# Turning q and k by the DMA crossbar in place of TensorE, in batches 2 to 7 of an attention and SwiGLU kernel

## The chip, the cores and the metric

The kernel runs on one core of one Trainium2 chip. The time is device microseconds (us) of that core, from the first to the last instruction, as the median of several runs. Runs of one kernel mostly agree within a few tenths of a per cent; a run over 1.5% above the fastest of the same kernel counts as slow and is left out of the ratios. A ratio is the mean time of one kernel's fast runs over the mean of the other's fast runs of the same rounds on the same chip, so it is not quite the ratio of the medians that are quoted beside it.

Names: PE is TensorE (PEld its weight loads), DVE is VectorE, ACT is ScalarE, POOL is GpSimd, SP is SyncE. ACTq, POOLq and SPq are the sequencers of those engines, which issue DMAs. "L123" is a line of the kernel; lines of the changed kernel stand about 17 higher than those of the kernel before.

## The reference, cut to what matters

```python
batch, n_heads, seq, head_dim = (8, 8, 576, 64)          # q, k: randn * 0.1
scores = scale * np.matmul(q, k.transpose(0, 1, 3, 2))   # scale = 1/8
scores = np.where(causal, -1e9, scores + decay)          # decay[i, j] = cum[i] - cum[j]
attn = softmax(scores)                                   # written out in the reference
x = np.matmul(attn, v)                                   # heads side by side: [4608, 512]
out = (silu(x @ w_gate) * (x @ w_val)) @ w_out           # d_ff = 1536
```

All inputs are float32. The score matmul contracts over head_dim, so q and k must lie with head_dim on the partitions, that is, turned.

Of the kernel before, what the change touches and what calls it, by code (L numbers as in the profile page):

```python
# [9 lines left out]
BF16 = mybir.dt.bfloat16  # L10
# [22 lines left out]
def kernel(ctx, tc, q, k, v, f, w_gate, w_val, w_out, out):  # L33
    nc = tc.nc
    B, H, S, D = q.shape
# [3 lines left out]
    P = 128  # L39
# [26 lines left out]
    ps_o = ctx.enter_context(tc.tile_pool(name="ps_o", bufs=1, space=PSUM))  # L66
    dec_dram = nc.dram_tensor("dec_d", (BH, 2, 4, S), BF16, kind="Internal").ap()
    rc_dram = nc.dram_tensor("rc_d", (BH // GH + AHEAD * H // GH, GH * S), F32, kind="Internal").ap()
    order = ctx.enter_context(tc.manual_schedule())

    NBUF = 4
    FB = H // 2

    QK = [consts.tile([KR, 4, NB * P], BF16, name=f"QK{i}") for i in range(NBUF)]

    BF = {(nm, i): consts.tile([P, QT, 2, D], BF16, name=f"b_{nm}{i}") for nm in "qk" for i in range(2)}
    VB = [consts.tile([P, NB, 2, P], BF16, name=f"VB{i}") for i in range(NBUF)]
# [7 lines left out]
    def load(p, nm, part=0):  # L85
        if nm != "v":

            t = natp.tile([QP, 2, QT * D], F32, name=f"nat_{nm}", tag=f"nat_{nm}")
            nc.sync.dma_start(
                out=t, in_=srcs[nm][2 * p : 2 * p + 2].rearrange("h (p t) d -> p h (t d)", t=QT)  # L90
            )
            nat[nm, p] = t
            return
        if part == 0:
            nat[nm, p] = natp.tile([P, NB, 2, D], F32, name="nat_v", tag="nat_v", bufs=3)
        t = nat[nm, p]
        if part < 2:
            nc.sync.dma_start(
                out=t[:, : NB - 1, part, :],
                in_=srcs[nm][2 * p + part, : (NB - 1) * P].rearrange("(n p) d -> p n d", p=P),  # L100
            )
        else:
            nc.sync.dma_start(
                out=t[:LAST, NB - 1],
                in_=srcs[nm][2 * p : 2 * p + 2, (NB - 1) * P :].rearrange("h p d -> p h d"),
            )

    def rows(p):
        nc.sync.dma_start(
# [44 lines left out]
    def qk(h, i):  # L154
        b, j = (h // 2) % NBUF, h % 2
        ahead = h < AHEAD * H and i == 0
        if ahead:
            PT[h, 0] = pt0p.tile([P, 2 * QSPLIT], BF16, name="pt0", tag="pt0")
        elif i == 0 or (h < AHEAD * H and i == 1):
            PT[h, 0] = PT[h, 1] = ptp.tile([P, PT_W], BF16, name="pt", tag="pt")  # L160
        pt = PT[h, min(i, 1)]
        pool, tag = (ps_ffn, "f") if h < H and ahead else (ps_s, "s")
        s = pool.tile([P, 512], F32, name="s", tag=tag)
        c = 0
        for kt, q0, w in BANKS[i]:
            nc.tensor.matmul(  # L166
                s[:, c : c + w], QK[b][:, 2 * j + 1, kt * P : (kt + 1) * P], QK[b][:, 2 * j, q0 : q0 + w],
                start=True, stop=True,
            )
            c += w  # L170
        off = OFFS[i]
        nc.scalar.activation(pt[:, off : off + c], s[:, :c], AF.Exp, scale=0.125)  # L172
        if i == 0:
            diag = pt[:, : 2 * QSPLIT].rearrange("p (n x) -> p n x", x=QSPLIT)[:, :, :P]
            pat = [[0, 2], [1, P]]
        else:
            kt, q0, w = [x for x in BANKS[i] if x[1] == x[0] * P][0]
            lo = off + sum(x[2] for x in BANKS[i][: [y[0] for y in BANKS[i]].index(kt)])
            m = min(P, w)
            diag, pat = pt[:, lo : lo + m], [[1, m]]  # L180
        nc.gpsimd.affine_select(  # L181
            out=diag, in_=diag, pattern=pat, compare_op=ALU.is_ge, fill=0.0, base=0, channel_multiplier=-1,
        )
# [140 lines left out]
    with tc.tile_pool(name="ini", bufs=1) as ini:  # L324
        lf = ini.tile([BH, S], F32, name="lf")
        nc.scalar.dma_start(out=lf, in_=f.rearrange("b h s -> (b h) s"))
        for p in range(2):
            load(p, "q")
            load(p, "k")
        for part in range(3):  # L330
            load(0, "v", part)
        for part in range(3):
            load(1, "v", part)
        load(2, "q")
        load(2, "k")
        ident = consts.tile([P, P], BF16, name="ident")
        make_identity(nc, ident[:, :])
        ident_f = consts.tile([P, P], F32, name="ident_f")
        zero = ini.tile([BH, S], F32, name="zero")
        dec = ini.tile([BH, 2, 4, S], BF16, name="dec")  # L340
        nc.gpsimd.memset(zero, 0.0)
        for n in range(2):
            nc.vector.memset(BF["q", n][QP:], 0.0)
            nc.vector.memset(BF["k", n][QP:], 0.0)
        nc.vector.memset(dec[:, 1, 0], 1.0)
        nc.gpsimd.memset(dec[:, 0, 1:], 1.0)
        blanks(0)
        cast(0, "q")
        cast(0, "k")
        nc.vector.tensor_scalar(out=lf, in0=lf, scalar1=1e-4, scalar2=1.0, op0=ALU.max, op1=ALU.min)  # L350
        nc.scalar.activation(lf, lf, AF.Ln)
        idle(7)
        transposes(0, "q")
        straighten(0, "q", 0, nc.scalar)
        straighten(0, "q", 1, nc.scalar)
        idle(2)
        cast(1, "q")
        cast(1, "k")
        cum = ini.tile([BH, S], F32, name="cum")

        def row(r):

            nc.sync.dma_start(out=QK[0][D + r : D + r + 1, :, :S], in_=dec[0:2, :, r])

        nc.vector.tensor_tensor_scan(out=cum, data0=lf, data1=zero, initial=0.0, op0=ALU.add, op1=ALU.add)
        nc.scalar.activation(dec[:, 0, 0], cum, AF.Copy, scale=8.0)
        row(0)
        nc.vector.tensor_scalar_mul(dec[:, 1, 1], cum, -8.0)
        row(1)
        transposes(0, "k")  # L370
        straighten(0, "k", 0, nc.scalar)
        straighten(0, "k", 1, nc.scalar)
        r1 = ini.tile([BH, S], F32, name="r1")
        nc.vector.scalar_tensor_tensor(out=r1, in0=cum, scalar=-8.0, in1=dec[:, 1, 1], op0=ALU.mult, op1=ALU.subtract)
        nc.vector.tensor_copy(dec[:, 1, 2], r1)
        row(2)
        nc.vector.tensor_sub(dec[:, 1, 3], r1, dec[:, 1, 2])
        row(3)
        nc.sync.dma_start(out=dec_dram[:H], in_=dec[:H])

        warm = ini.tile([1, 1], F32, name="warm")
        nc.scalar.activation(warm, cum[:1, :1], AF.Exp)
        idle(4)
        transposes(1, "q")
        straighten(1, "q", 0, nc.scalar)
        straighten(1, "q", 1, nc.scalar)
        idle(2)
        cast(0, "v")
        transposes(1, "k")
        straighten(1, "k", 0, nc.vector)  # L390
        straighten(1, "k", 1, nc.vector)
        idle(3)
        load(3, "q")
        load(3, "k")
        for part in range(3):
            load(2, "v", part)
        rows(1)
        rows(2)
        rows(3)
        cast(2, "q")  # L400
        cast(2, "k")
        blanks(1)
        nc.gpsimd.tensor_copy(ident_f, ident)
        blanks(2)
        nc.sync.dma_start(out=dec_dram[H:], in_=dec[H:])
    fp = ctx.enter_context(tc.tile_pool(name="fp", bufs=3))
# [52 lines left out]
    for p in range(NP):  # L459
        s0 = slot(2 * p, 0)  # L460
        if p >= AHEAD * FB:
            l, r = s0 - 20, s0 - 16
            cq, tq, ck, tk, cv = s0 - 12, s0 - 8, s0 - 8, s0 - 4, s0 - 4
        elif p >= FB:

            e = slot(2 * (p - NBUF) + 1, NSLOT - 1)
            l = (4, 7, 15, 19)[p - FB]
            r = e + 1
            tq = max(18 + 4 * (p - FB), e)
            tk = tq + 2  # L470
            cq, ck = tq - 4, tk - 4
            cv = e + LAG + 1
            lv = 8 + 5 * (p - FB)
        else:
            if p > 1:
                for nm, t in (("q", s0 - 3), ("k", s0 - 2)):
                    if p > 2:
                        at(s0 - 5, cast, p, nm)
                    at(t, transposes, p, nm)
                    for a in range(2):  # L480
                        at(t + a, straighten, p, nm, a, nc.scalar if nm == "q" else nc.vector)
            if p > 0:
                at(s0, cast, p, "v")
            continue
        for n, (nm, part) in enumerate((("q", 0), ("k", 0), ("v", 0), ("v", 1), ("v", 2))):
            at(l + n + n // 2 if p >= AHEAD * FB else l if n < 2 else lv, load, p, nm, part)
        at(r, rows, p)
        for nm, c, t in (("q", cq, tq), ("k", ck, tk)):
            at(c, cast, p, nm)
            at(t, transposes, p, nm)  # L490
            for a in range(2):
                at(t + a, straighten, p, nm, a, nc.scalar if nm == "q" else nc.vector)
        at(cv, cast, p, "v")
# [69 lines left out]
```

## The kernel before: what the change and the argument touch

Work goes by head pairs (32 of them, `p`), and by slots: each slot is one bank of scores of one head, and FFN matmuls of an earlier batch fill PE between slots. `at(slot, fn, ...)` puts a step into the program order of its engine at that slot. A pair has 8 slots, and `s0` is its first.

Before, q and k of a pair are loaded in float32 by SP, cast to bf16 by POOL, turned by PE into PSUM (six transposes for a pair's q, six for its k) and copied into the operand by ACT and DVE. Four extra rows of the operand (64 to 67) hold the decay, loaded by `rows`.

```python
QK = [consts.tile([KR, 4, NB * P], BF16, name=f"QK{i}") for i in range(NBUF)]   # KR = 68, NBUF = 4

def rows(p):
    nc.sync.dma_start(out=QK[p % NBUF][D:KR, :, :S], in_=dec_dram[...])

def transposes(p, nm):
    ...
    for n in range(QT):                                   # QT = 6
        nc.tensor.transpose(t[:, n * QP : n * QP + P], src[:, n], ident)

def straighten(p, nm, a, eng):                            # PSUM to operand, on ACT or DVE
    ...
```

The second part is the chain that divides by the softmax sums, once for every four heads. Its three DMAs are issued by ACT:

```python
def collect(x, g, lo, n):      # sums of four heads to 128 partitions
    nc.scalar.dma_start(out=SC[x][:, :c], in_=E[g][D : D + 1, ...])
def recip(x, n):
    nc.vector.reciprocal(RC[x][:, :c], SC.pop(x)[:, :c])
def back(x, n):                # reciprocals to DRAM
    nc.scalar.dma_start(out=rc_dram[x, : GH * n]..., in_=RC.pop(x)[:, :c])
def spread(x, n):              # broadcast of 576 KB to 64 partitions
    nc.scalar.dma_start(out=RB[x][:, : GH * n], in_=rc_dram[x, : GH * n]...to_broadcast(...))
def normalise(...):            # DVE: xT = ev * rb; the FFN of that batch waits for xT
    ...
```

One fact about the program that the source does not show, but its list of waits does: the framework gives the DMAs of the two hardware queues, SP's and ACT's together, eight completion semaphores in turn. Before a DMA is issued, its sequencer waits until the DMA that used the same semaphore last, eight DMAs back in program order, has landed. DMAs issued by POOL have eight others.

The softmax here doesn't subtract the row's maximum and nothing guards it: scores larger than these inputs give would overflow.

## Time and profile before

| | before |
|---|---|
| time, median | 451.91 us (451.03 to 453.86, 3 runs) |
| PE busy | 418.1 us, 93% of the span |
| DVE, ACT, POOL busy | 64%, 59%, 39% |
| granted PE clock, mean | 0.973 |

The page's second part cuts the span into 40 slices; a digit is the busy share in tenths. For the kernel before:

```profile
PE   8399587899899899999999999999999999999996
...
PEclk9758999999999999999999999999999999999999
DMA  9899960762818644942594359425912222200201
```

After the first fifth PE is full nearly everywhere. The table by stretches of time says it in numbers (columns: stretch, its length, busy us of PE, PEld, DVE, ACT and POOL with counts, granted clock, DMA share, GB/s; a DMA share adds up the times of all packets over 16 engines, so it can pass 1):

```profile
core 0: us, PE busy (x) PEld busy (x) DVE busy (x) ACT busy (x) POOL busy (x), PEclk, DMA share, GB/s
...
155.00:200.00 45.00, 43.40 (x312) 25.67 (x310) 32.57 (x56) 32.56 (x69) 23.36 (x54) 1.00 0.56 133
200.00:245.00 45.00, 45.00 (x306) 25.74 (x305) 31.41 (x51) 31.73 (x65) 20.29 (x48) 1.00 0.55 132
245.00:290.00 45.00, 45.00 (x308) 25.77 (x306) 31.32 (x51) 31.72 (x66) 20.27 (x48) 1.00 0.55 132
```

PE is busy 45.00 of 45 us, DVE and ACT about 31, the others less: PE is the limit here. What one group of six transposes costs PE is read from the timeline (start, length, engine, line):

```profile
202.98 0.50 PE L135 MATMUL tp<-ident,b_k 128*128 128x128 bf16 x6
203.32 0.81 PE L293 MATMUL gp<-xT,wg 128*128 128x512 bf16 x3
```

The group is listed as 0.50 us, but the next matmul starts 0.34 us after its first: the rest overlaps.

### The profile page before, as it was taken

To read this page: it belongs to the slowest core of one execution; us is meant where nothing else is said; L and a number is where in the kernel's file an instruction comes from. 1 tells how busy PE (TensorE), PEld (TensorE's weight loads), DVE (VectorE), ACT (ScalarE), POOL (GpSimd) and SP (SyncE) were. 2 spreads that over 40 slices of the span, in tenths; PEclk is the share of its full clock that TensorE was granted. 3 is DMA by queue.
4 is the path that set the end of the run, shared out by engine and by line. 5 is a ranking of instruction groups with operands and counts; after the bars stand their busy time and mean duration, and the time that the engine had idled before them with its cause. 6 is when DMAs were issued, how large, how long until landed. Compare 5 with 4: busy or idle time off the path is not lost.

```text
span 449.0 us, 8044 instructions
## 1 busy us (share of the span) xinstructions
PE 418.1 (93%) x2818; PEld 248.2 (55%) x2818; DVE 289.1 (64%) x523; ACT 267.1 (59%) x551; POOL 174.6 (39%) x409
## 2 busy tenths in 40 slices
PE   8399587899899899999999999999999999999996
PEld 3256465676766565555555555555555554444562
DVE  6464466585866875797379737973796479386280
ACT  5446466666667778776677667766776643233231
POOL 7855654334245646444444444444444310000000
PEclk9758999999999999999999999999999999999999
DMA  9899960762818644942594359425912222200201
GB/s 210 175 231 202 223 142 12 196 142 49 193 55 197 149 110 131 213 95 70 154 208 99 69 155 205 102 70 153 207 29 64 88 54 54 85 10 1 93 2 70
DMA packets 70195, 53.52 MB, mean 119 GB/s; under 512 B 45834, under 2 KB 64266, under 8 KB 69322
## 3 DMA queue, kind: packets, MB, share of 16 engines
q1 hardware_dynamic: 57626, 38.94, 35.0%
q10 hardware_dynamic: 6704, 9.34, 8.9%
q0 software_dynamic: 5824, 4.72, 6.8%
q8 instruction: 22, 0.36, 0.4%
q14 instruction: 19, 0.16, 0.1%
HBM read 47.38 MB, written 10.17 MB: 128 GB/s over the span
## 4 chain that ended last, share of the span: by engine, by line
PE 75%; DMA 9%; DVE 7%; ACT 4%; issue 2%; SPq 1%; ACTq 1%; POOL 0%; DVEq 0%; POOLq 0%
PE fo L311 20%; PE gp L293 18%; PE vp L302 18%; PE o L198 8%; PE s L166 8%; PE tp L135 4%; DMA nat_q<-in_q_dram 3%; DMA nat_v<-in_v_dram 3%; DVE th L296 2%; DVE xT L274 2%; DMA sc<-ev 2%; DVE hh L304 1%; ACT th L295 1%; ACT QK L142 1%; ACT pt L172 1%
## 5 line engine op out<-in xcount | busy, mean ns | idle before, releaser
L172 ACT ACTIVATE pt<-s 128x384 bf16<-128x384 f32 (+2 forms) x256 | 127.6, 502 | 77.1 <-PE s L166 72.0
L181 POOL TENSOR_SCALAR_AFFINE_SELECT pt<-pt 128x128 bf16<-128x128 bf16 (+2 forms) x256 | 83.8, 328 | 180.3 <-ACT pt L172 177.1
L302 PE MATMUL vp<-xT,wv 128*128 128x512 bf16 (+2 forms) x528 | 125.4, 341 | 1.4 <-DVE hh L304 1.4
L293 PE MATMUL gp<-xT,wg 128*128 128x512 bf16 (+2 forms) x528 | 125.9, 342 | 0.8 <-DVE th L296 0.5
L296 DVE SCALAR_TENSOR_TENSOR th<-th,gp 128x512 f32<-128x512 f32 (+2 forms) x132 | 77.5, 587 | 66.6 <-ACT th L295 63.6
L311 PE MATMUL fo<-wo,hh 128*128 128x512 bf16 x432 | 107.2, 379 | 0.8 <-DVE th L296 0.8
L166 PE MATMUL s<-QK 68*128 68x320 bf16 (+4 forms) x448 | 88.5, 268 | 8.8 <-DMA QK<-dec_d 5.8
L295 ACT ACTIVATE th<-gp 128x512 f32<-128x512 f32 (+2 forms) x132 | 68.3, 517 | 47.1 <-PE gp L293 39.0
L198 PE MATMUL o<-pt,VB 128*128 128x320 bf16 (+4 forms) x448 | 88.0, 267 | 5.6 <-DVE QK L144 2.6
L304 DVE TENSOR_TENSOR hh<-th,vp 128x512 bf16<-128x512 f32 (+2 forms) x132 | 77.5, 587 | 9.3 <-PE vp L302 0.7
L166 PEld LDWEIGHTS <-QK 68*128 68x128 bf16 x448 | 44.4, 101 | 49.4 <-issue 8.1
L302 PEld LDWEIGHTS <-wv 128*128 128x128 bf16 x528 | 49.3, 98 | 33.5 <-issue 2.4
L293 PEld LDWEIGHTS <-wg 128*128 128x128 bf16 x528 | 49.4, 98 | 32.2 <-issue 1.2
L219 DVE COPY ev<-o 65x320 f32<-65x320 f32 (+1 forms) x68 | 32.5, 478 | 42.2 <-PE o L198 42.1
L311 PEld LDWEIGHTS <-hh 128*128 128x128 bf16 x432 | 39.3, 97 | 35.6 <-issue 1.2
L144 DVE COPY QK<-tp 64x576 bf16<-64x576 bf16 x62 | 46.6, 752 | 17.7 <-PE tp L135 16.9
L198 PEld LDWEIGHTS <-VB 128*128 128x128 bf16 x448 | 39.2, 98 | 23.2 <-issue 4.9
L142 ACT ACTIVATE QK<-tp 64x576 bf16<-64x576 bf16 x66 | 42.6, 645 | 13.5 <-DMA nat_q<-in_q_dram 4.0
L274 DVE TENSOR_TENSOR xT<-ev,rb 64x576 bf16<-64x576 f32 (+2 forms) x72 | 48.6, 675 | 2.9 <-DMA rb<-rc_d 1.9
L314 ACT ACTIVATE ot<-fo 128x512 f32<-128x512 f32 x36 | 21.5, 596 | 29.9 <-PE fo L311 28.3
L122 POOL CAST b_q<-nat_q 96x768 bf16<-96x768 f32 x32 | 27.1, 846 | 6.7 <-DMA nat_q<-in_q_dram 6.7
L122 POOL CAST b_k<-nat_k 96x768 bf16<-96x768 f32 x32 | 27.0, 843 | 0.9 <-DMA nat_k<-in_k_dram 0.9
(49 smaller groups left out, 176.2 us busy)
## 6 DMA issues: line engine op xcount, KB each, us to landing
nat_q<-in_q_dram SPq DMA_DIRECT2D x32, 288.0 KB, 3.8
nat_k<-in_k_dram SPq DMA_DIRECT2D x32, 288.0 KB, 4.2
out_dram<-ot SPq DMA_DIRECT2D x36, 256.0 KB, 2.1
nat_v<-in_v_dram SPq DMA_DIRECT2D x64, 128.0 KB, 5.7
rb<-rc_d ACTq DMA_DIRECT2D x12, 576.0 KB, 6.8
wg<-in_moe_w_gate_dram POOLq DMA_DIRECT2D x4, 384.0 KB, 13.2
wv<-in_moe_w_val_dram POOLq DMA_DIRECT2D x4, 384.0 KB, 15.2
wo<-in_moe_w_out_dram POOLq DMA_DIRECT2D x4, 384.0 KB, 9.6
```

The lines of the kernel that those rows point to most:

```text
L122: nc.gpsimd.tensor_copy(BF[nm, p % 2][:QP].rearrange("p t h d -> p h t d"), nat.pop((nm, p)).rearrange("p h (t d) -> p h t d", d=D),)
L166: nc.tensor.matmul(s[:, c : c + w], QK[b][:, 2 * j + 1, kt * P : (kt + 1) * P], QK[b][:, 2 * j, q0 : q0 + w], start=True, stop=True,)
L172: nc.scalar.activation(pt[:, off : off + c], s[:, :c], AF.Exp, scale=0.125)
L181: nc.gpsimd.affine_select(out=diag, in_=diag, pattern=pat, compare_op=ALU.is_ge, fill=0.0, base=0, channel_multiplier=-1,)
L198: nc.tensor.matmul(o[:, q0 - q_lo : q0 - q_lo + w], VB[b][:, kt, j, :], PT[h, half][:, c : c + w], start=(i <= 1 and n == 0), stop=(last a ...
L274: nc.vector.tensor_mul(xT[a * D : (a + 1) * D, (h % H) // 2, b0 : b0 + n], E[g][:D, c : c + n], RB[x][:, j * n : (j + 1) * n])
L293: nc.tensor.matmul(g_[:, :n], wg[:, ko, fs], xT[:, ko, ts], start=(ko == 0), stop=(ko == KD - 1))
L295: nc.scalar.activation(th[:, :n], g_[:, :n], AF.Tanh, scale=0.5)
L296: nc.vector.scalar_tensor_tensor(out=th[:, :n], in0=th[:, :n], scalar=1.0, in1=g_[:, :n], op0=ALU.add, op1=ALU.mult)
L302: nc.tensor.matmul(v_[:, :n], wv[:, ko, fs], xT[:, ko, ts], start=(ko == 0), stop=(ko == KD - 1))
L304: nc.vector.tensor_mul(h_[:, :n], th[:, :n], v_[:, :n])
L311: nc.tensor.matmul(o[:m], hh[fc][:, m0 : m0 + m], wo[:, fc, :], start=(fc == 0), stop=(fc == KF - 1))
```

## The change

The intent is to take these transposes off PE. For batches 2 to 7, POOL issues two DMAs per batch that cast all of q and of k to bf16 in DRAM (`narrow`), and SP issues four crossbar transposes per pair (`turned`) that write the operand directly. The loads of q and k, the casts on POOL, the PE transposes and the copies on ACT and DVE go away. The crossbar takes rows of 128 elements, and a row of one head has 64, so each transpose reads half a row too many and writes partitions 64 to 127 with data that nobody needs. `rows` then overwrites partitions 64 to 67, so it now has to wait until the transposes have landed.

```diff
+    qk_dram = nc.dram_tensor("qk_d", (2 * B, H * S * D + D), BF16, kind="Internal").ap()
-    QK = [consts.tile([KR, 4, NB * P], BF16, name=f"QK{i}") for i in range(NBUF)]
+    QK = [consts.tile([P, 4, NB * P], BF16, name=f"QK{i}") for i in range(NBUF)]
+    def narrow(b, x):
+        src = (q, k)[x]
+        nc.gpsimd.dma_start(
+            out=qk_dram[2 * b + x, : H * S * D].rearrange("(a c) -> a c", c=2048),
+            in_=src[b].rearrange("h s d -> (h s d)").rearrange("(a c) -> a c", c=2048),
+        )
+    def turned(p, j):
+        b, h = divmod(2 * p + j, H)
+        for x in range(2):
+            lo = (2 * b + x) * (H * S * D + D) + h * S * D
+            src = bass.AP(qk_dram.tensor, qk_dram.offset + lo, [[D, S], [1, P]])
+            nc.sync.dma_start_transpose(out=QK[p % NBUF][:, 2 * j + x, :S], in_=src)
 ...
         if p >= AHEAD * FB:                      # batches 2 to 7
-            l, r = s0 - 20, s0 - 16
-            cq, tq, ck, tk, cv = s0 - 12, s0 - 8, s0 - 8, s0 - 4, s0 - 4
+            l = s0 - 20
+            if p % FB == 0:                      # first pair of a batch
+                for x in range(2):
+                    at(l - 6, narrow, p // FB, x)
+            for part in range(3):
+                at(l + part, load, p, "v", part)
+            for j in range(2):
+                at(s0 - 12 + 2 * j, turned, p, j)
+            at(s0 - 8, rows, p)
+            at(s0 - 4, cast, p, "v")
+            continue
```

Left out of the diff: the operand slices `[:KR]` in the score matmul, and a small zero fill at the end of each DRAM row.

More of the change, by code (lines that the diff above doesn't have):

```diff
@@ L166, in qk @@
             nc.tensor.matmul(
-                s[:, c : c + w], QK[b][:, 2 * j + 1, kt * P : (kt + 1) * P], QK[b][:, 2 * j, q0 : q0 + w],
+                s[:, c : c + w], QK[b][:KR, 2 * j + 1, kt * P : (kt + 1) * P], QK[b][:KR, 2 * j, q0 : q0 + w],
                 start=True, stop=True,
@@ L403 @@
         nc.gpsimd.tensor_copy(ident_f, ident)
+        edge = ini.tile([2 * B, D], BF16, name="edge")
+        nc.gpsimd.memset(edge, 0.0)
+        nc.sync.dma_start(out=qk_dram[:, H * S * D :], in_=edge)
         blanks(2)
```

## The prediction

> **What bounds the kernel now.** TensorE (PE). The stretch table shows PE busy 45.00 of 45 us in 200 to 245, 245 to 290 and 290 to 335 us at a granted clock of 1.00; DVE and ACT are busy about 31.5 of 45 us, DMA about 55%. From 90 us on the list of waits gives PE under 5 us. The last 83 us are FFN matmuls alone. Before 60 us DMA is full (share 1.08); the change does not touch that part.
>
> **What it removes (24 head pairs).** 288 of the 384 transposes. A group of six shows 0.50 us in the timeline, but the next matmul starts 0.33 to 0.34 us after the group's first (202.98 to 203.32), so a group holds PE for 0.336 us; 48 groups make 16.1 us. The page's busy sum (34.2 us for 384) would say 25 us, too much, I think, since pipelined ends overlap the next matmul. Also 48 casts on POOL (0.845 us), 48 copies on DVE and ACT (0.75 and 0.65): off the critical path, but they free DVE and ACT, and the PSUM tile that transposes share with attention outputs; 1 to 2 us of PE waits in 110 to 200 us should go too. And 48 loads of 288 KB, about 14 us of full DMA per batch[...].
>
> **What it adds.** Per batch two DRAM-to-DRAM casts (2.36 MB read, 1.18 MB written). The weight casts wrote 4.72 MB in a 6.8% share of 449 us, 155 GB/s: estimate 7.6 us of full DMA per batch. Per batch 16 crossbar transposes of 576x128 bf16 (147 KB, half of it not used). No transpose is in this trace. The Trainium skill, "DMA: Bandwidth & Descriptors", section on latency and measured facts, gives 261 GB/s for one kernel: estimate 0.57 us each, 9 us per batch. DMA then stays near 55%. At twice that or more, a pair's four transposes still fit the 11.2 us that a pair lasts; above about 2 us each DMA saturates.
>
> **Critical path.** Only the 16 us of PE and the small waits. A pair's first transpose is issued 12 slots (16.8 us at 1.4 us a slot) before use, the cast 14 slots (19.6 us) before that, so latency should be hidden. The first cast falls near 72 us, where DMA is almost idle (0.11). The danger is the softmax-sum chain: its broadcast (rb) lands after 6.8 us and is needed about 7 us after issue, so queueing behind casts or transposes becomes a DVE wait, and DVE feeds PE. I take 2 to 4 us back for that.
>
> **Time.** 451.9 - 16 - 2 + 3 = about 437 us, 3.3% faster. Range 429 to 458. Faster by over 2% 0.66, within 2% 0.20, slower by over 2% 0.14.
>
> **What would show it.** Right: the pair period in the steady part falls from 11.2 to about 10.5 us with PE still at 100%; DMA share 50 to 65%; transposes landing in 2 to 4 us; scores never wait for QK; the FFN tail still about 83 us. Wrong: PE idle before the scores, released by QK transposes; SP waiting long at the transposes or at the row loads behind them; DVE waiting for rb; DMA share near 100%.
>
> **What would make it wrong.** A transpose that occupies the queue for 2 us or more; casts that take over 20 us under contention, so that the in-order SP queue holds up v loads and output stores behind the first transpose; a broadcast delayed by several us per batch. On the other side, if the busy sum is the truer cost, 428 us.

## The result, and the profile after

| | before | after |
|---|---|---|
| time, median | 451.75 us (4 runs) | 495.13 us (490.74 to 495.89, 4 runs) |
| ratio of the fast runs | | 1.0935 (95%: 1.0884 to 1.0987) |
| PE busy | 418.1 us, 93% | 414.8 us, 84% |
| granted PE clock, mean | 0.973 | 0.918 |

The change is 9.3% slower. The page's slices after:

```profile
PE   7499686979598839994999299947999999999996
...
PEclk9658987999799979998899689996999999999999
DMA  9899917665758677967688646885485430310201
```

PE now has holes in the part where it was full, and the granted clock dips behind them. The same stretches as above:

```profile
155.00:200.00 45.00, 32.59 (x215) 19.54 (x215) 19.18 (x37) 21.64 (x51) 14.46 (x41) 0.92 0.79 146
200.00:245.00 45.00, 37.58 (x209) 19.79 (x212) 23.62 (x38) 21.27 (x47) 13.25 (x37) 0.92 0.77 136
245.00:290.00 45.00, 35.09 (x201) 18.84 (x203) 21.96 (x37) 21.26 (x46) 11.42 (x34) 0.89 0.76 145
```

DMA is at 77%, not full, and every engine has become idler at once. The holes are few and long. From the starts of the first mask of each head, a pair took 11.21 us before (median, from 195 us on). After, the median is 10.54 us, which is what was hoped for, but the mean is 12.52: most pairs run faster, and some stand still.

Who stands first? The list of waits from 110 to 410 us (engine and line, waited for, us in total, times, longest), kernel after:

```profile
PE s L183 <- ACT pt L189: 34.2, 6, 9.7
ACT th L312 <- DMA QK<-qk_d: 31.9, 3, 11.9
ACT pt L189 <- DMA QK<-qk_d: 9.5, 1, 9.5
```

PE waits for ACT's exp, and ACT, which touches no operand of the scores, waits for the transposes that write it. The timelines of one of these stalls show how. ACT first, then DVE, SP and PE:

```profile
268.93 0.49 ACT L189 ACTIVATE pt<-s 128x384 bf16<-128x384 f32 x1
280.96 0.32 ACTq L278 DMA_DIRECT2D rc_d<-rc  x1
281.32 0.60 ACT L312 ACTIVATE th<-gp 128x512 f32<-128x512 f32 x1 [11.90 <-DMA QK<-qk_d]
```

```profile
269.50 0.26 DVE L274 RECIPROCAL rc<-sc 128x18 f32<-128x18 f32 x1
...
281.95 0.69 DVE L313 SCALAR_TENSOR_TENSOR th<-th,gp 128x512 f32<-128x512 f32 x1 [11.58 <-ACT th L312]
```

```profile
266.38 2.50 SPq L123 DMA_TRANSPOSE QK<-qk_d  x2
268.92 0.62 SPq L104 DMA_DIRECT2D nat_v<-in_v_dram  x1
277.89 0.28 SPq L126 DMA_DIRECT2D QK<-dec_d  x1
278.21 2.45 SPq L123 DMA_TRANSPOSE QK<-qk_d  x2
```

```profile
272.39 0.38 PE L319 MATMUL vp<-xT,wv 128*128 128x512 bf16 x1
282.46 0.43 PE L183 MATMUL s<-QK 68*128 68x320 bf16 x1 [9.69 <-ACT pt L189]
```

The reciprocals were ready at 269.76 us. ACT is next to issue their store to DRAM (L278), and issues it only at 280.96. The trace's DMA records say what the store waited for: its completion semaphore is number 102, the user before it is the transpose that SP issued at 278.21, and that one landed at 280.88. SP issued that transpose late because it stood at the row load (L126) from 269.5 to 277.9, until the pair's last transpose, issued at 267.62, had landed at 277.75, 10.1 us after its issue. The chain of waits runs through the same points (start, length, what):

```profile
267.62 10.13 DMA QK<-qk_d
...
277.89 0.28 SPq L126
...
278.21 2.67 DMA QK<-qk_d
...
280.96 0.32 ACTq L278
...
281.32 0.60 ACT th L312
```

Over the whole trace from 90 us on, ACT stands 12 times over 1 us at a DMA issue, 60.2 us together (counted from the end of ACT's work before the issue to the issue); in the kernel before it is twice, 3.1 us. In 11 of the 12, the issue came within 0.2 us after the landing of the last user of the same semaphore, which was a transpose or a v load of SP.

And why did that transpose need 10 us, when the median lands in 3.2? The casts of the next batch were issued at 267.70 and 268.22. The DMA view of an equal moment one batch earlier (casts issued at 217.19 and 217.71), for 216 to 220 us and then for 220 to 224 us (queue, packets, MB, share of 16 engines; q0 is POOL's queue, q1 SP's; for 216 to 220 us SP's line alone):

```profile
q1 hardware_dynamic: 1664, 0.41, 47.7%
```

```profile
q0 software_dynamic: 63, 0.87, 109.7%
q1 hardware_dynamic: 92, 0.02, 3.6%
```

While the casts run, SP's queue moves 92 packets in 4 us in place of 1,664. The Trainium skill, "DMA: Bandwidth & Descriptors", section on queues, rings and completion order, says that an engine goes round its queues packet by packet; the counts here agree in kind (92 against 63). A transfer of the casts is 18,432 bytes and takes 1.38 us (median of 384); a 256-byte packet of SP's queue, as a row of a transpose is, takes 18 ns (median). So a transpose of 576 rows stands behind the casts until they are done. It happens once at each of the five bursts that meet transposes: one transpose each lands in 9.0 to 10.1 us.

The stall is not over when ACT goes on: in 234 to 239 us of this trace, after another stall of 8 us, the granted clock is 0.57 and PE starts 19 matmuls in 5 us, against 26 in the next 4 us at a clock of 1.00. The Trainium skill, "TensorE: Matmul & The Clock Gate", section "Why this matters for your kernels", warns of PE gaps above about 3 us for this reason. This trace agrees for its five gaps of 6.0 to 9.7 us after 90 us: a stretch at half clock begins 3.0 to 4.5 us after the start of each. It shows no sharp limit: a gap of 2.5 us (from 104.95 us) was followed by such a stretch too, and one of 2.9 us (from 158.32) was not.

So the first theory, called C, is: ACT is blocked at its own DMA issues by completion semaphores that it shares with SP's transposes, and SP issues those late. Rivals: D, the crossbar is too slow and the scores wait for it; K, the casts alone do the harm through the queues, and the semaphores are only where it shows.

### The profile page after: what moved, and what is told of

Same layout as the page of the kernel before. It is cut to its first block, busy times and chain, and to the rows that moved or that the text cites. A ratio compares the mean times of both kernels' runs of the same rounds, so it can differ in the third digit from the quotient of the medians.

```text
span 492.9 us, 7426 instructions
## 1 busy us (share of the span) xinstructions
PE 414.8 (84%) x2497; PEld 237.6 (48%) x2530; DVE 255.5 (52%) x475; ACT 236.1 (48%) x503; POOL 142.4 (29%) x374
## 4 chain that ended last, share of the span: by engine, by line
PE 60%; DMA 27%; DVE 4%; ACT 2%; SPq 2%; issue 2%; ACTq 1%; POOL 0%; POOLq 0%; DVEq 0%
PE fo L328 18%; PE gp L310 14%; PE vp L319 14%; DMA QK<-qk_d 12%; DMA nat_v<-in_v_dram 8%; PE s L183 7%; PE o L215 6%; DMA nat_q<-in_q_dram 4%; DMA rb<-rc_d 1%; DMA sc<-ev 1%; DVE xT L291 1%; DVE th L313 1%; ACT th L312 1%; ACT pt L189 1%; DVE hh L321 1%
## 5 line engine op out<-in xcount | busy, mean ns | idle before, releaser
L310 PE MATMUL gp<-xT,wg 128*128 128x512 bf16 (+2 forms) x523 | 128.4, 349 | 9.1 <-DVE th L313 8.5
L183 PE MATMUL s<-QK 68*128 68x320 bf16 (+4 forms) x448 | 91.1, 275 | 47.7 <-ACT pt L189 35.7
L319 PE MATMUL vp<-xT,wv 128*128 128x512 bf16 (+2 forms) x517 | 127.4, 348 | 0.7 <-DVE hh L321 0.3
L215 PE MATMUL o<-pt,VB 128*128 128x320 bf16 (+4 forms) x448 | 91.3, 275 | 6.6 <-DVE ev L236 4.3
L310 PEld LDWEIGHTS <-wg 128*128 128x128 bf16 x528 | 50.8, 100 | 42.4 <-issue 10.5
L215 PEld LDWEIGHTS <-VB 128*128 128x128 bf16 x448 | 40.7, 101 | 60.2 <-issue 44.4
L319 PEld LDWEIGHTS <-wv 128*128 128x128 bf16 x528 | 50.8, 100 | 34.6 <-issue 2.9
L234 ACT ACTIVATE ev<-o 65x256 f32<-65x256 f32 x52 | 19.4, 374 | 2.5 <-DVE xT L291 1.3
L136 POOL CAST VB<-nat_v 128x512 bf16<-128x512 f32 x28 | 17.6, 628 | 0.0
L161 DVE COPY QK<-tp 64x576 bf16<-64x576 bf16 x14 | 10.5, 753 | 8.7 <-PE tp L152 8.5
L159 ACT ACTIVATE QK<-tp 64x576 bf16<-64x576 bf16 x18 | 11.6, 644 | 6.3 <-DMA nat_q<-in_q_dram 3.3
```

The costliest lines, as they stand in the source:

```text
L183: nc.tensor.matmul(s[:, c : c + w], QK[b][:KR, 2 * j + 1, kt * P : (kt + 1) * P], QK[b][:KR, 2 * j, q0 : q0 + w], start=True, stop=True,)
L215: nc.tensor.matmul(o[:, q0 - q_lo : q0 - q_lo + w], VB[b][:, kt, j, :], PT[h, half][:, c : c + w], start=(i <= 1 and n == 0), stop=(last a ...
L310: nc.tensor.matmul(g_[:, :n], wg[:, ko, fs], xT[:, ko, ts], start=(ko == 0), stop=(ko == KD - 1))
L319: nc.tensor.matmul(v_[:, :n], wv[:, ko, fs], xT[:, ko, ts], start=(ko == 0), stop=(ko == KD - 1))
```

## The experiments

"e" kernels are edits of the changed kernel, "b" of the kernel before. The correctness check says little here: q and k are drawn with a factor of 0.1, so scores are small, and kernels whose score operands are wrong pass too. Executed numerically in a simulator (no time taken from it), the relative error of the output is 0.0049 for before, after and e13_pool_pair alike, and 0.0143 for e1_no_crossbar with its stale operands.

### 1. How much the change could gain: no transposes, and neither casts nor transposes

```diff
-            for j in range(2):
-                at(s0 - 12 + 2 * j, turned, p, j)
```

e1_no_crossbar leaves the casts in:

> The change without its crossbar transposes (the casts stay, the scores of batches 2 to 7 read stale operands, so the result is wrong on purpose). This is the ceiling of the change. If six transposes hold TensorE 0.336 us, 48 groups are 16 us and the time is 433 to 438 us; if the page's busy sum of 25 us is the truer cost, 425 to 429 us. If the casts alone harm, it stays above 445 us.

Measured: 442.19 us (before in the same rounds 451.90), ratio 0.9778.

e8_neither also drops the two lines that call `narrow`.

> The change with neither casts nor crossbar transposes (stale operands, wrong on purpose): the bare saving of TensorE time and of the q and k loads. If 0.336 us a group is right, 433 to 437 us, and the run with casts alone (442.19 us) showed 5 to 9 us of harm by the casts. If it comes out at 440 to 443 us too, the casts cost nothing and the 16 us were oversized.

Measured: 431.66 us (before 451.76), ratio 0.9548. The stretch of 200 to 245 us in e8_neither:

```profile
200.00:245.00 45.00, 45.00 (x275) 24.51 (x274) 27.65 (x45) 28.44 (x61) 15.35 (x42) 1.00 0.35 88
```

PE is full again, and the gain is 20.1 us, a little more than the range given. The pair period is 10.54 us, 0.67 less than before, and that is two groups of 0.336 us. The prediction's 16 us of transposes were sound, its 2 us of waits close (4 us are left when the 16 are taken from the gain), and the page's busy sum (25 us) too high. The casts alone take back 10.5 us: in e1_no_crossbar ACT stands 5.3 us at a broadcast whose reciprocals reach DRAM late behind a cast, and PE loses time in 60 to 90 and in 155 to 200 us (22.89 and 40.43 us busy, against 25.47 and 45.00).

### 2. The chain's DMAs off ACT, with its control

```diff
 def collect / back / spread:
-    nc.scalar.dma_start(
+    (nc.gpsimd if x > 1 else nc.scalar).dma_start(
```

This is e3_chain_pool. POOL's DMAs have semaphores of their own, so neither ACT's nor the chain's issues wait for SP's transposes any more.

> The sums chain's DMAs (collect, back, spread) from the third chain on issued by GpSimd, whose software DMAs have completion semaphores of their own. Theory C: ACT no longer stands 7 to 11 us at a DMA issue, time 435 to 450 us. Theory K or D: the chain still lands late and DVE or the scores wait instead, 475 to 495 us.

Measured: 457.98 us (before 451.90), ratio 1.0121. 37 us of the 63 between the change and its ceiling (e8_neither) are back, more than K or D allow, though the time is above the range that C gave (one of the four runs counts as slow). ACT's waits over 1 us at a DMA issue after 90 us are gone. The waits that are left, e3_chain_pool, 90 to 410 us:

```profile
PEld L183 <- DMA QK<-dec_d: 23.0, 5, 6.4
DVE xT L291 <- DMA rb<-rc_d: 22.8, 7, 9.7
PE s L183 <- DMA QK<-dec_d: 20.6, 5, 5.9
```

Now the scores wait for the row loads, which stand behind the transposes, and DVE waits for the broadcast. PE and PEld stand idle here over the same five waits, so they are 23 us and not 43: two expectations below count them twice.

The control is b1_chain_pool:

> The control: the kernel before with the sums chain's DMAs on GpSimd as in e3_chain_pool. Theory C says that the kernel before loses under 4 us at ACT's DMA issues, so 447 to 453 us: the gain of e3_chain_pool is then the removal of a cost that the change brought. If this also falls by 10 us or more, the chain on ACT was a cost of both kernels.

Measured: 455.73 us (before 451.76), ratio 1.0085, a little above the range given. In the kernel before, the same move costs about 4 us. The gain in e3_chain_pool is therefore the removal of a cost that the change had brought. The move changes three things at once: ACT no longer issues the chain's DMAs, these use POOL's semaphores, and they run on POOL's queue. No run takes these apart; that ACT stood for the semaphores is read from the trace above.

### 3. Transposes without the later casts, with the chain on either engine

```diff
-            if p % FB == 0:
+            if p == AHEAD * FB:                  # cast batch 2 only
 ...
-            lo = (2 * b + x) * (H * S * D + D) + h * S * D
+            lo = (2 * AHEAD + x) * (H * S * D + D) + h * S * D
```

This is e5_one_cast, with the chain on ACT:

> The change with the casts of batch 2 alone; all later transposes read that batch's rows (wrong on purpose). Transposes and everything else stay. Theory K (the cast packets start every stall): 440 to 455 us. Theory C (semaphores shared with transposes, SP issuing late) with the casts only as a trigger of some stalls: 465 to 485 us.

Measured: 461.81 us (before 451.76), ratio 1.0198, a little under C's range and above K's. Transposes alone cost 30 us over the ceiling, with ACT standing 28 us at its DMA issues. Two transposes landed late here with no cast under way: those issued at 172.5 and 173.7 us took 11.9 and 10.9 us, beside a broadcast of the chain, issued at 172.6, that took 11.4 us where no other took over 7.0. Why was not found out.

e12_pool_one_cast is the same with the chain on POOL:

> Transposes with the casts of batch 2 alone (wrong on purpose) as in e5_one_cast (461.81 us), but the chain on GpSimd. Theory C (most of what transposes cost passes through ACT's semaphore waits): 436 to 447 us. If transposes cost by their own lateness: 452 to 460 us.

Measured: 439.95 us (before 451.29), ratio 0.9744. The same transposes, now 22 us faster because the chain has left ACT. PE is full (45.00 of 45 us in three of four stretches from 155 us on) at a DMA share of 65 to 78%. The stretch of 155 to 200 us, e5_one_cast and then e12_pool_one_cast, at nearly the same DMA share:

```profile
155.00:200.00 45.00, 34.48 (x213) 19.74 (x212) 19.17 (x35) 21.65 (x50) 12.73 (x39) 0.92 0.72 123
```

```profile
155.00:200.00 45.00, 43.65 (x284) 24.85 (x283) 29.93 (x51) 29.98 (x65) 21.93 (x57) 1.00 0.71 144
```

Theory D falls here: with ACT decoupled and no bursts, the crossbar delivers in time, and it costs 8 us over the ceiling, of which the control puts about 4 on the chain's move.

Put together (medians; the ceiling is 431.66):

| | chain on ACT | chain on POOL |
|---|---|---|
| casts only | 442.19 (+10.5) | |
| transposes, one batch cast | 461.81 (+30.2) | 439.95 (+8.3) |
| both | 495.13 (+63.5) | 457.98 (+26.3) |

With the chain on ACT, both together cost 23 us more than the sum of each alone: the casts delay the transposes, and the semaphores carry the delay into ACT. The semaphores are not the whole of it: all casts add 33 us to the transposes with the chain on ACT, and still 18 with it on POOL. Casts alone with the chain on POOL were not run.

### 4. What about the casts: the length of their packets, or the burst?

e2_small_packets makes the casts' runs 384 elements long, so transfers of 768 bytes at 79 ns:

```diff
-            out=qk_dram[2 * b + x, : H * S * D].rearrange("(a c) -> a c", c=2048),
+            out=qk_dram[2 * b + x, : H * S * D].rearrange("(n a c) -> a n c", a=128, c=384),
```
(and the source in the same way.)

> The casts in runs of 384 elements, so packets near 768 bytes in place of 18432. Theory K (the casts' packets of 1.38 us hold every ring, so that the transposes and the sums chain behind them land 8 to 10 us late once per batch, and this starts the stalls): 440 to 455 us. Theory C (the ACT engine waits at its own DMA issues for completion semaphores that transposes on SP used last, because SP issues those late): only part is gone, 460 to 480 us. Theory D (the crossbar itself is too slow): 485 to 495 us.

Measured: 488.70 us (before 451.90), ratio 1.0816: 6 us better than the change, and within what D had for it. Taken alone this run would have spoken for D. Its trace shows why short packets help so little. From 126 to 130 us, while casts run:

```profile
q0 software_dynamic: 761, 0.57, 91.1%
q1 hardware_dynamic: 752, 0.19, 35.8%
```

The two queues take turns packet by packet, and SP's moves 752 in place of the 92 above. But a burst is now 1,536 packets in place of 64, and the transposes issued at 122.8 and 124.2 us landed in 11.1 and 10.0 us, as late as with long packets.

e10_pair_casts casts per pair, in transfers of 9,216 bytes, two DMAs every 8 slots:

```diff
-            if p % FB == 0:
-                for x in range(2):
-                    at(l - 6, narrow, p // FB, x)
+            for x in range(2):
+                at(l - 6, narrow, p, x)
 ...
-            out=qk_dram[2 * b + x, : H * S * D].rearrange("(a c) -> a c", c=2048),
+            out=qk_dram[2 * b + x, h * S * D : (h + 2) * S * D].rearrange("(a c) -> a c", c=1152),
```

> The change with the casts cut into one per head pair (packets of 9216 bytes, two casts every 8 slots in place of a burst per batch), chain left on ACT. If the burst starts the long stalls: 465 to 480 us, and no ACT wait over 6 us. If only the bytes count, or the semaphores alone: 488 to 498 us.

Measured: 475.61 us (before 451.29; two of its four runs count as slow), ratio of the fast runs 1.0421. 20 us better than the change. ACT's longest stand at a DMA issue is 5.9 us (6.4 in the list of waits, which counts up to ACT's next work, so that "no wait over 6 us" holds or narrowly fails by the count used). The semaphore waits are still there, but shorter and more: 18 over 1 us, 55.5 us together, against 12 and 60.2. Their sum hardly fell, so it is not the sum that sets the time; the long waits are gone.

e13_pool_pair is this with the chain on POOL:

> Chain on GpSimd and casts per pair, row loads on SP at their first place. The burst of casts is the trigger: 440 to 450 us, a win over the kernel before. If the bytes of the casts[...] cost wherever they fall: 454 to 462 us, as e3_chain_pool.

Measured: 440.14 us (before 451.55), ratio 0.9752 (95%: 0.9719 to 0.9784). Casts per pair and the chain on POOL beat the kernel before by 2.5%, with correct operands.

e16_pool_small has the short packets of e2_small_packets with the chain on POOL:

> Chain on GpSimd, casts in bursts per batch, but in packets near 768 bytes. In the change's trace SP's queue moves some 15 packets a microsecond while the casts run, one for each packet of theirs, against 700 or more alone. If that alternation with 1.38 us packets is what hurts: 438 to 448 us against 457.98 with long packets. If the burst as such hurts (the bytes, 47 us of ring time at this packet size against 37): 455 to 465 us.

Measured: 463.71 us (before 451.82), ratio 1.0249. With ACT decoupled and the burst kept, short packets do not help; the time is no better than with long ones (457.98).

e17_pool_pair_small:

> As e13_pool_pair (440.14 us), with packets near 768 bytes as well. If packet length still matters at 9216 bytes: 433 to 438 us. If not: 438 to 444 us.

Measured: 442.61 us (before 451.82), ratio 0.9800. The same as e13_pool_pair within the runs' spread. So it is the burst, two DMAs that write 1.18 MB at once, and not the length of a packet.

### 5. Where the row loads stand, and how early things start

e4_rows_late moves `rows` from `s0 - 8` to `s0 - 3`, so that SP issues the next pair's first transposes before it stands at the rows.

> The row loads 3 slots before use in place of 8, so that SP does not stand at them until the transposes just issued have landed, and the next pair's transposes go out first. If SP standing there is what makes the semaphores come late (theory C, SP as cause): 445 to 465 us. If the crossbar or the casts are at fault by themselves: 485 to 500 us.

Measured: 493.86 us (485.4 to 501.33, two of four runs slow; before 451.90), ratio of the fast runs 1.0784: a miss for SP's standing as the cause by itself. ACT's waits at DMA issues after 90 us fall from 60 to 23 us, but the rows now come too late. e4_rows_late, 90 to 410 us:

```profile
PEld L183 <- DMA QK<-dec_d: 23.6, 9, 8.8
...
PE s L183 <- DMA QK<-dec_d: 19.9, 6, 8.5
```

e6_pool_rows is the same with the chain on POOL:

> Chain on GpSimd and row loads 3 slots before use. In e3_chain_pool the scores waited 43 us for the rows, which wait for the transposes and stand in SP's order. If SP standing at the rows delays everything behind them: 440 to 452 us. If the transposes themselves come too late (the queue's rate): 455 to 468 us, with the wait for the rows still there.

Measured: 473.50 us (before 451.76), ratio 1.0492: 15 us worse than with the rows at their first place.

e9_pool_rows4 and e11_pool_rows_pair issue the rows from POOL at `s0 - 4` (with the chain on POOL; e11 also with casts per pair).

> Chain on GpSimd (as e3_chain_pool, 457.98 us), and the row loads of batches 2 to 7 also from GpSimd, 4 slots before use, so that SP never stands at them. If SP standing at the rows is the rest of the loss: 442 to 452 us and no wait of the scores for the rows. If the queues are slow by themselves (casts, broadcast and transposes in one another's way): 454 to 465 us.

Measured: 496.41 us (before 451.29), ratio 1.0973. In its profile, of a slow run, PE waits 46 us before the scores for the rows, which now stand in POOL's order behind the chain.

> All three: chain and rows on GpSimd, casts per pair. If these three account for the loss, it beats the kernel before: 434 to 447 us, against the ceiling of 431.66 us without casts and transposes. If something else of the crossbar costs TensorE time: 450 us or more.

Measured: 480.82 us (before 451.29), ratio 1.0581. e13_pool_pair is this kernel with the rows left on SP at `s0 - 8`, and 41 us faster. With the chain on POOL all three runs with moved rows are slower than with the rows at their first place; e4_rows_late, with the chain on ACT, is level with the change or slightly faster (ratio 1.0784 against 1.0935). So the rows were in a good place. The runs do not say that SP's standing costs nothing, since each of them made the rows late as well; that part stays open.

e14_pool_early and e15_pool_pair_early start casts, transposes and rows 8 slots earlier.

> Chain on GpSimd, casts in bursts per batch, but casts, transposes and row loads 8 slots (about 11 us) earlier. If what is left in e3_chain_pool is latency (a 10 us delay of transposes and rows per burst, more than the lead): 440 to 448 us, and the scores wait under 10 us for the rows in place of 43. If it is a rate that SP or the rings can't hold: 454 to 462 us.

Measured: 470.52 us (before 451.55; two slow runs), ratio of the fast runs 1.0324. A miss for both readings.

> Both. If burst and lead are the whole rest: 436 to 445 us, close to e12_pool_one_cast (439.95 us). If casts cost beside that: 448 us or more.

Measured: 458.60 us (before 451.55), ratio 1.0144; this is in the range of the second reading (448 us or more). Both are worse than the same kernels at the first places (457.98 and 440.14), so a longer lead is not what was missing. In the trace of e14_pool_early one burst took 16 to 18 us to land, and transposes issued with it 19 to 20; ACT then waits for output stores (22.7 us in 90 to 410 us). Why the earlier places collide worse was not found out.

## Why the prediction was wrong, point by point

- **PE is the limit, and the transposes are worth 16 us, the waits 2.** Right. The ceiling run gained 20.1 us, and a group's 0.336 us was the better reading than the busy sum. The pair period of about 10.5 us came true as the median after, 10.54 us, but not PE at 100% with it.
- **DMA load.** Off in two terms. The loads of q and k that go away are 9,216 transfers of 1,536 bytes that took 53 us of full DMA in all, 8.8 us per batch; the prediction's 14 us was wrong arithmetic (14.1 MB are the loads of all six batches, not of one). A transpose was put at 0.57 us from the 261 GB/s of the skill; its packets took 87 us in 96 transposes, 0.91 us each, 163 GB/s (the 256-byte packets of SP's queue took 140.8 us after and 53.7 before, all of them loads of v; the difference is the transposes'). The casts, estimated at 7.6 us per batch, took 6.2. So DMA load rose by about 12 us per batch and not by 3, and its share to 77% and not 50 to 65%. This is not the cause of the loss: e12_pool_one_cast runs at 75% with PE full.
- **"Only the 16 us of PE and the small waits" lie on the critical path, and latency is hidden.** This is the step that failed. Latency was reckoned from each transfer to its own consumer, and there it held: in the change the scores wait only 8.3 us for rows from DRAM, in two waits, and one of these, 5.4 us at the start, is in the kernel before too (5.8). What it left out is that DMA issues tie engines together. ACT issues three DMAs per chain in order with exp and tanh, and each first waits for the last user of its completion semaphore. After 90 us ACT stood 60.2 us at 12 of these issues; at 9 of them the last user was a transpose of SP, at 2 a load of v. e3_chain_pool (37 us back), its control (4 us lost) and e12_pool_one_cast (22 us back with no bursts) show it.
- **The danger is the softmax-sum chain.** The right chain, the wrong link. The prediction expected DVE to wait for the broadcast, 2 to 4 us. DVE's waits for it came to 6.7 us; ACT's at its DMA issues came to 60.
- **"Casts that take over 20 us".** They landed in 8.3 us (median of twelve), well inside their lead, and still did harm: in those us SP's queue moved a few per cent of its packets, so one transpose at each burst, issued within 1.3 us of a cast, landed in 9.0 to 10.1 us in place of 3.2. That the SP sequencer would stand at the row loads was named as a sign, and seen: 55.2 us.
- **The FFN tail of 83 us.** Right: 78.19 us of PE work in the last 83 us, against 79.09 before.

Settled: the larger part of the loss against the ceiling (37 of 63 us) passes through ACT's DMA issues, where ACT stands for semaphores that transposes which land or are issued late used last; a burst of casts makes the loss twice as large (30 us with the casts of one batch, 63 with all). Open: whether other semaphores alone, with ACT still issuing, would have been enough; how much of SP's standing at the rows could be saved by itself; and why starting earlier is worse.

## What to carry to other kernels

Before moving work to a DMA queue, list every engine that issues DMAs and ask what it would have to wait for at the issue: not only its data, but the semaphore, and so the slowest DMA that shares it. An engine with work on the critical path should issue no DMA whose semaphore it shares with long or late transfers. Cut a large DRAM-to-DRAM transfer into pieces spread over the time it serves, and look at the landing times of the other queues while it runs.

## What the Trainium skill lacked or had wrong

- "Trainium Kernel Development and Optimization", key constraints, says that issuing DMAs from several engines concurrently only saves the sequencer's issue time. Here moving three DMAs per chain from ACT to GpSimd moved the time from 495.13 to 457.98 us, and ACT's 60.2 us of standing at its DMA issues were gone with it.
- "DMA: Bandwidth & Descriptors", section on why a DMA increments its semaphore by 16, advises one semaphore per DMA in flight. It does not say what a shared pool costs when semaphores are waited for before reuse: 60.2 us of ACT standing at its issues.
- The same page gives 261 GB/s for a crossbar transpose and 350 to 400 GB/s for the contiguous case. Here 96 transposes of 576x128 bf16 in 256-byte rows, which overlap by half, took 87 us of full DMA beside other transfers, 163 GB/s, and each held SP's sequencer for 1.25 us (median).
- The same page, rules for kernel authors, says, of what must be serialised, that a transpose next to ordinary DMAs needs nothing. It does not speak of time: behind a burst of casts a transpose landed in 10.1 us in place of 3.2.
- No page has the cost of a casting DRAM-to-DRAM DMA: 589,824 bytes written took 18,432-byte transfers of 1.38 us each and landed in 8.3 us (median of twelve, two at a time).
